# Expert 0's first product from the slot table of twelve tiles, with a branch that recomputes it, and weight loads placed in time by VectorE writes

## The chip, the cores and the metric

The kernel runs on one core of a Trainium2 chip. Five engines work from queues of their own and wait for one another through semaphores: TensorE (PE in the rows; its weight loads are PEld), VectorE (DVE), ScalarE (ACT), GpSimd (POOL) and SyncE (SP), which here only issues DMAs. An engine takes its instructions in the order in which the program gives them. The metric is the device time of one launch in microseconds (us).

## The reference, cut to what matters

Attention in chunks of 64 positions gives 2,304 tokens of 512 numbers. A first mixture of eight experts sends each token to the expert with the largest logit, in the order of the tokens, up to 576 for an expert. A second mixture, which takes most of the time, applies eight experts to every token.

```python
    x = np.ascontiguousarray(attn_out.transpose(0, 2, 1, 3)).reshape(B * S, H * D)
    ...
    logits = x @ w_gate
    expert_idx = np.argmax(logits, axis=1)
    ...
    for i in range(N):
        e = expert_idx[i]
        if counts[e] < capacity:
            disp[e, counts[e]] = x[i]
    ...
    h = np.maximum(np.einsum('ecd,edf->ecf', disp, w1), 0.0)
    y = np.einsum('ecf,efd->ecd', h, w2)
```

`w1[e]` is 512 x 1024 and `w2[e]` 1024 x 512. The next expert's input can't be known before the tokens have been routed.

## The kernel before, in words

The program is written out in the order in which each engine is to work (a manual schedule); nothing reorders it later. Where an operation's data isn't there, its engine waits, and everything behind it on that engine waits too.

**Attention and routing.** The loop `for n in range(NT + 6)` (NT = 18 tiles of 128 tokens) runs stages of several tiles interleaved: in iteration `n`, stage `f` works on tile `n - lag`. `order` lists the stages. Rows of attention output, split into a high and a low half of 16 bits, are written to the DRAM tensor `xs_d`, 512 numbers and eight more with the token's gate. After each group of three tiles (`G = 3`, six groups) `route(g)` gives the parts of the routing: one-hot of the chosen expert, `r_mm` (ranking by matmuls into the bank `p_tab`), `r_sel` to `r_ci`, rows and columns of a table, `r_tab` (three matmuls that put token numbers into slots) and `r_acc`, which adds them up in `tacc`. After the last group the sum becomes `gidx`, the list of tokens of each expert by slot, and `reg_i`, the counts and ranks.

**First mixture.** For expert `x`, `blocks(x, ...)` does 256 tokens at once: rows gathered from `xs_d` by indirect DMA on GpSimd's queue, turned, then a first product in four pieces of 24 matmuls (each matmul 256 columns), and a second product of 24 matmuls (512 columns) for each tile of 128 tokens. Weights and inputs are split into a high and a low half, so a product has three terms. Each piece is emptied from its PSUM bank by ScalarE (`hh`) and VectorE (`hl`); each tile of the second product by a square, a scale and a row write. The call with `main=True` does the first 256 tokens; the late block does tokens 256 to 511 where there are that many, behind `tc.If(rc > 256)`; the rest is a loop. `sites` are places in `blocks` (one behind each piece and one behind each tile) at which other work is put in.

**Weights.** Ahead of expert x's products its matrices "a" (`w1`) and "b" (`w2`) are loaded by `w_load` on SyncE's queue, their sizes are taken by `w_stat` ("a" by squares on ScalarE, "b" by maxima `wmxb` on VectorE), a common scale is made by `w_scale` (matmuls into `p_sum`) and `w_scale2`, and `w_split` writes high and low halves. Expert `x + 1` is split and the matrices of `x + 2` are measured while `x` runs. For expert 0, the loads of expert 1 are issued in iteration `NT + 1`, those of expert 2 ahead of `blocks(0, ...)`, and its late rows are turned (`xTc`) between first and second product (`between`).

Of the kernel before, what the change touches and what calls it, by code (L numbers as in the profile page):

```python
# [30 lines left out]
def kernel(ctx, tc, q, k, v, w_gate, w1, w2, capacity, w2_gate, w21, w22, out):  # L31
    nc = tc.nc
# [119 lines left out]
    def w_load(x, nm, h, nh=2):  # L152
# [152 lines left out]

    ohsum = [const.tile([128, E], F16, name=f"ohsum{j}") for j in range(2)]
# [4 lines left out]
    with ExitStack() as actx:  # L311
# [5 lines left out]
        ps_t = actx.enter_context(tc.tile_pool(name="ps_t", bufs=3, space=PSUM))  # L317
# [56 lines left out]
        def st_tr(i):  # L374
# [3 lines left out]
            for h2 in range(2):  # L378
                p = ps_t.tile([128, PR, 128], F32, tag="t", name="p_t")
# [29 lines left out]
        def st_dtr(i):  # L409
            d = T[i].pop("d")  # L410
            p = ps_t.tile([128, PR, 128], F32, tag="t", name="p_t")
# [51 lines left out]
        def st_xtr(i):  # L463
            p = ps_t.tile([128, KD, 128], F32, tag="t", name="p_t")
# [163 lines left out]
        for nm, ld, st, sc, sp in (("a", (2, 3), (3, 4, 5, 6), 6, (10, 13, 8, 15)), ("b", (9, 10), (11, 10, 12, 12), 12, (15, 14, 16, 17))):  # L628
            for h in range(2):
                plan(ld[h], lambda nm=nm, h=h: w_load(0, nm, h))  # L630
                plan(NT + 1, lambda nm=nm, h=h: w_load(1, nm, h))
# [4 lines left out]
            for h in range(4):  # L636
# [3 lines left out]
                 (st_max, 2), (st_xcopy, 4), (st_tr, 0), (st_pv, 3), (st_logits, 5), (st_dtr, 2))  # L640
        todo_r = {}
        for n in range(NT + 6):
# [9 lines left out]
            if i >= 0 and i % G == G - 1 and i < NT - G:  # L652
                for m, part in zip((n, n + 1, n + 1, n + 3, n + 5), route(i // G)):
                    todo_r.setdefault(m, []).append(part)
# [8 lines left out]
            for f, lag in order:  # L663
                i = n - lag
                if 0 <= i < NT:
                    f(i)
                for r in queue[:share]:
# [8 lines left out]
        for r in [gw, eps, rec, sel, pos, kx, rout, *second, *tab, tot1, tot2, racc]:  # L676
            r()

# [7 lines left out]
        nc.vector.tensor_copy(reg_i[:, 0:2 * E], p_tab[:, 256:256 + 2 * E])  # L686
    small_pool.pop()


    ps = ctx.enter_context(tc.tile_pool(name="ps", bufs=1, space=PSUM))  # L690
    turns = {"p": [0, 1, 2], "y": [3, 4], "c": [5, 6]}

    def in_turn(kind, shape, dtype, nm):
        i = turns[kind].pop(0)
        turns[kind].append(i)
        return ps.tile(shape, dtype, tag=f"m{i}", name=nm)

    with ExitStack() as cctx:
# [4 lines left out]
        sums["bank"] = ps.tile([128, 512], F32, tag="l", name="p_sum")  # L703
# [21 lines left out]
        def turn(rows, tag, bank="y"):  # L725
            xT = cp.tile([128, 2 * KD, 128 * len(rows)], F16, tag=tag, name=tag, bufs=2 if tag == "xT" else 1)
            for n, (idx, kg, xg) in enumerate(rows):
                p = in_turn(bank, [128, 2 * KD, 128], F16, "p_t")
                for kk in range(2 * KD):
                    nc.tensor.transpose(p[:, kk, :], xg[:, kk * 128:(kk + 1) * 128], id16)  # L730
                sl = slice(n * 128, (n + 1) * 128)
                nc.scalar.copy(out=xT[:, 0:KD, sl], in_=p[:, 0:KD])
                nc.vector.tensor_copy(xT[:, KD:2 * KD, sl], p[:, KD:2 * KD])
# [4 lines left out]
        def blocks(x, pre, nb, row0, sites=(), main=False, between=None):  # L738
            a, b = mats[x, "a"], mats[x, "b"]
# [14 lines left out]
            hh = cp.tile([128, KF, 256], F16, tag="hh", name="hh", bufs=1)[:, :, 0:W]  # L754
            hl = cp.tile([128, KF, 256], F16, tag="hl", name="hl", bufs=1)[:, :, 0:W]
            FG = 512 // W
            for fg in range(KF // FG):
                p = bank("p", [128, FG, W])
                for f4 in range(FG):
                    f = fg * FG + f4  # L760
                    n = 0
                    for w, lo in ((a.hi, 0), (a.hi, KD), (a.lo, 0)):
                        for kk in range(KD):
                            nc.tensor.matmul(p[:, f4, :], lhsT=w[:, kk, f * 128:(f + 1) * 128], rhs=xT[:, lo + kk, 0:W],  # L764
                                             start=(n == 0), stop=(n == 3 * KD - 1))
                            n += 1
                fs = slice(fg * FG, fg * FG + FG)
                nc.scalar.activation(out=hh[:, fs, :], in_=p, func=AF.Relu)
                nc.vector.scalar_tensor_tensor(out=hl[:, fs, :], in0=p, scalar=0.0, in1=hh[:, fs, :],
                                               op0=ALU.max, op1=ALU.subtract)  # L770
                site()
# [37 lines left out]
        def loads(x, nm, lo=0, hi=4):  # L809
            for h in range(lo, hi):  # L810
                w_load(x, nm, h, 4)
# [16 lines left out]
        first = gather(tokens(0, 0, 1))  # L828
        late = gather(tokens(0, 2, 3))
        rows = gather(tokens(1, 0, 1))  # L830
        for f in stats(1):
            f()
        pre = turn(first, "xT")

        for x in range(E):
            y = x + 1
            rc = nc.values_load(reg_i[0:1, x:x + 1], min_val=0, max_val=N)
# [9 lines left out]

            cur, pre = pre, turn_dma(rows) if y < E else None
            late_cur, late = late, gather(tokens(y, 2, 3)) if y < E else None
            rows = gather(tokens(y + 1, 0, 1)) if y + 1 < E else None  # L850
            if x == 0:
# [567 lines left out]
```

## Time and profile before

| | us |
|---|---|
| median of 3 runs | 1795.99 |
| the three runs | 1797.54, 1788.5, 1795.99 |
| the profiled execution | 1796.67 |
| its span, first to last instruction | 1795.0 |
| attention and routing, until gidx | 140.9 |
| first mixture, until its last second product | 413 |

[...] In rows with a time, the first number is the start in us from the span's start and the second the duration, or the stretch that several alike instructions fill; the bracket says how long the engine was idle before, and what ended that.

### The profile page before, as it was taken

How to read it: one execution, taken by the hardware profiler on the slowest of the kernel's cores; microseconds unless marked ns; L12 is line 12 of the kernel's file. 1: busy time of each engine (PE TensorE's matmuls, PEld its weight loads, DVE VectorE, ACT ScalarE, POOL GpSimd, SP SyncE). 2: the span in 40 equal slices, each digit the busy share in tenths (PEclk: the TensorE clock that was granted, in tenths of full speed). 3: DMA queues.
4: the chain of work that ended last, by engine and by line, in shares of the span. 5: the costliest groups of instructions: out<-in, count | busy, mean ns of one | idle time of the engine just before them, and what ended most of it. 6: DMA issues, size and time to landing. Idle time of an engine off the chain costs nothing.

```text
span 1795.0 us, 32982 instructions
## 1 busy us (share of the span) xinstructions
PE 1706.4 (95%) x13011; PEld 1234.3 (69%) x13011; DVE 1202.0 (67%) x2340; ACT 955.1 (53%) x1806; POOL 729.9 (41%) x754
## 2 busy tenths in 40 slices
PE   7887999988999999999999999999999999999995
PEld 6765667665555477777777777777777777777674
DVE  4897557756467666776678667677766786676652
ACT  7965557655245455564366445555643665453440
POOL 1345335542021345353455344453534553443432
PEclk9987999999999999999999999999999999999997
DMA  9747678943324322332324224223323142231200
GB/s 236 208 157 208 153 197 198 234 115 121 108 65 149 122 96 91 109 131 82 130 62 171 90 82 156 97 101 112 126 87 130 62 171 75 97 124 63 97 36 35
DMA packets 140902, 219.15 MB, mean 122 GB/s; under 512 B 62880, under 2 KB 81392, under 8 KB 140720
## 3 DMA queue, kind: packets, MB, share of 16 engines
q1 hardware_dynamic: 133728, 198.92, 35.1%
q0 software_dynamic: 5360, 17.24, 3.5%
q8 instruction: 115, 1.88, 0.4%
q10 hardware_dynamic: 1632, 0.56, 0.1%
q14 instruction: 67, 0.55, 0.1%
HBM read 167.56 MB, written 41.91 MB: 117 GB/s over the span
## 4 chain that ended last, share of the span: by engine, by line
PE 66%; DVE 7%; ACT 2%; DMA 1%; issue 1%; POOLq 0%; DVEq 0%; ACTq 0%
PE p_m L1122 35%; PE p_m L1210 27%; PE p_m L1254 3%; DVE wall L290 3%; ACT wall L289 1%; DVE acc L1189 1%; DMA wb_d<-wall 1%; DMA out_dram<-acc,rk 1%; DVE xsum L971 1%; DVE el L1130 1%; DVE tq L1137 0%; ACT eh L1127 0%; PE p_m L1010 0%; ACT tq L1162 0%; DVE wall L248 0%
## 5 line engine op out<-in xcount | busy, mean ns | idle before, releaser
L1122 PE MATMUL p_m<-x,wall 128*128 128x384 f16 x4032 | 669.6, 327 | 8.2 <-ACT tq L1162 4.9
L1210 PE MATMUL p_m<-wall,eh 128*128 128x256 f16 x3528 | 580.3, 273 | 0.0
L1122 PEld LDWEIGHTS <-wall 128*128 128x128 f16 x4032 | 394.8, 98 | 268.6 <-issue 15.2
L1134 POOL TENSOR_TENSOR el<-tq,eh 128x384 f16<-128x384 f32 x336 | 344.4, 1053 | 558.8 <-ACT eh L1127 558.6
L1210 PE MATMUL p_m<-wall,el 128*128 128x256 f16 x1764 | 481.0, 273 | 1.2 <-DVE el L1130 1.2
L1127 ACT ACTIVATE eh<-tq 128x384 f16<-128x384 f32 x540 | 273.9, 522 | 194.9 <-DVE tq L1140 102.8
L1210 PEld LDWEIGHTS <-eh 128*128 128x128 f16 x3528 | 344.3, 98 | 44.3
L1189 DVE SCALAR_TENSOR_TENSOR acc<-p_m,cf,acc 128x256 f32<-128x256 f32 (+1 forms) x378 | 175.1, 521 | 128.0 <-PE p_m L1210 128.0
L1137 DVE TENSOR_TENSOR tq<-p_m,tq 128x384 f32<-128x384 f32 x288 | 158.5, 556 | 138.4 <-PE p_m L1122 137.2
L1210 PEld LDWEIGHTS <-el 128*128 128x128 f16 x1764 | 172.6, 98 | 21.5 <-DVE el L1130 1.5
L1130 DVE SCALAR_TENSOR_TENSOR el<-tq,eh 128x384 f16<-128x384 f32 x204 | 175.7, 864 | 10.0 <-ACT eh L1127 8.6
L1140 DVE SCALAR_TENSOR_TENSOR tq<-tq 128x384 f32<-128x384 f32 x252 | 133.3, 554 | 2.9
L764 PEld LDWEIGHTS <-wall 128*128 128x128 f16 x1152 | 108.2, 101 | 30.5 <-issue 16.8
L1162 ACT COPY tq<-p_m 128x384 f32<-128x384 f32 x96 | 45.7, 476 | 111.1 <-PE p_m L1122 108.6
L764 PE MATMUL p_p<-xT,wall 128*128 128x256 f16 x768 | 90.6, 280 | 7.8 <-PEq L896 4.3
L268 POOL TENSOR_TENSOR tq<-stb 128x256 f32<-128x256 f32 x56 | 50.1, 895 | 90.3 <-DVE wsumsq L184 70.4
L1254 PE MATMUL p_m<-wall,eh 128*128 128x512 f16 x288 | 85.6, 379 | 0.0
L1175 ACT ACTIVATE tq<-tq 128x384 f32<-128x384 f32 x84 | 43.9, 523 | 69.9 <-DVE tq L1137 69.9
L289 ACT ACTIVATE wall<-stb,wsb 128x256 f16<-128x256 f32 (+1 forms) x56 | 31.3, 605 | 93.3 <-DMA wb_d<-wall 67.9
L268 POOL TENSOR_TENSOR tq<-sta 128x256 f32<-128x256 f32 x56 | 45.0, 804 | 76.8 <-DVE wall L290 44.3
L290 DVE SCALAR_TENSOR_TENSOR wall<-stb,wsb,wall 128x256 f16<-128x256 f32 (+1 forms) x56 | 38.4, 698 | 51.2 <-ACT wall L289 48.6
L240 POOL TENSOR_SCALAR stb<-stb,wsb 128x1024 f32<-128x1024 f32 x16 | 52.8, 3299 | 40.9 <-ACT wall L239 37.7
(261 smaller groups left out, 2133.2 us busy)
## 6 DMA issues: line engine op xcount, KB each, us to landing
x<-xt_d SPq DMA_DIRECT2D x147, 384.0 KB, 3.6
sta<-in_moe_w_dram SPq DMA_DIRECT2D x18, 1024.0 KB, 6.6
stb<-in_moe_w_dram SPq DMA_DIRECT2D x18, 1024.0 KB, 7.9
wb_d<-wall SPq DMA_DIRECT2D x20, 896.0 KB, 3.6
wall<-wb_d SPq DMA_DIRECT2D x20, 896.0 KB, 6.4
sta<-in_moe_w_dram SPq DMA_DIRECT2D x28, 512.0 KB, 8.0
stb<-in_moe_w_dram SPq DMA_DIRECT2D x28, 512.0 KB, 6.7
xt_d<-x SPq DMA_DIRECT2D x21, 384.0 KB, 3.6
```

Source lines behind the costliest of these rows:

```text
L268: nc.gpsimd.tensor_tensor(out=at(o), in0=at(u), in1=at(v), op=op)
L290: nc.vector.scalar_tensor_tensor(out=o[:, cs, 1], in0=src, scalar=m.s, in1=o[:, cs, 0], op0=ALU.mult, op1=ALU.subtract)
L764: nc.tensor.matmul(p[:, f4, :], lhsT=w[:, kk, f * 128:(f + 1) * 128], rhs=xT[:, lo + kk, 0:W], start=(n == 0), stop=(n == 3 * KD - 1))
L1122: nc.tensor.matmul(p, lhsT=wt[:, w, lw, kk, :], rhs=xt[:, lx, kk, :], start=first and n == 0, stop=n == 5, skip_group_check=not first)
L1127: nc.scalar.activation(out=hs[op][0][:, q, :], in_=src, func=AF.Relu if op in (A11, A12, A22) or plain else AF.Copy)
L1130: nc.vector.scalar_tensor_tensor(out=hs[op][1][:, q, :], in0=src, scalar=0.0, in1=hs[op][0][:, q, :], op0=ALU.max, op1=ALU.subtract)
L1134: nc.gpsimd.tensor_tensor(out=hs[op][1][:, q, :], in0=src, in1=hs[op][0][:, q, :], op=ALU.subtract)
L1137: nc.vector.tensor_tensor(out=o, in0=a, in1=b, op=ALU.add)
L1140: nc.vector.scalar_tensor_tensor(out=o, in0=a, scalar=0.0, in1=b, op0=ALU.max, op1=op)
L1189: nc.vector.scalar_tensor_tensor(out=acc[:, j, cols], in0=y, scalar=coefs[x][:, j:j + 1], in1=acc[:, j, cols], op0=ALU.mult, op1=ALU.add)
L1210: nc.tensor.matmul(bk.t[:, cols], lhsT=hs[op][lh][:, q, t * 128:(t + 1) * 128], rhs=b.q[q][:, w, lw, :], start=m in (1, 5) and q == 0 and ...
L1254: nc.tensor.matmul(y.t, lhsT=h[:, kk % 4, c * 128:(c + 1) * 128], rhs=w[:, kk, :], start=(n == 0), stop=(n == 3 * KF - 1))
```

## The change

Three things, all up to the last expert of the first mixture.

1. *The table of twelve tiles.* After the fourth of six groups (`EG = NG - 3`) its table is made in iteration 19 and not 20 to 22, `tacc` is cast to indices, and the rows of the first 256 slots of expert 0 are gathered from the part of `xs_d` that the first twelve tiles wrote. They are turned at the end of iteration NT + 3. The four pieces of expert 0's first product stand in iterations NT + 4 and NT + 5 and between the last steps of the routing. `first_product` and `turn_into` are the old code as functions, the first one a generator that gives the emptying of each piece as a call.
2. *The branch.* `e_count` keeps how many of the first 1,536 tokens chose expert 0. If that is at most 255, the first 256 tokens are done again, in two blocks of 128. So `blocks(0, ...)` has only the two sites behind the tiles of the second product; the splits of expert 1 and the measures of expert 2 are put there, and turning the late rows comes behind.
3. *The writes.* `w_load(..., behind_vector=True)` has VectorE write one column of the destination before the load, so that the load can't start before VectorE has come to that place. Loads of later experts are spread over the sites, one of 512 KB at a time.

```diff
+        if behind_vector:
+            nc.vector.memset(m.st[:, h * c, 0:1], 0.0)
         nc.sync.dma_start(out=m.st[:, h * c:(h + 1) * c, :],
...
+    early = wall[:, 2 * 4096:4 * 4096]
+    e_rows = [wall[:, t * 2 * XW:(t + 1) * 2 * XW].bitcast(F32) for t in range(2)]
+    EG = NG - 3
...
-                plan(NT + 1, lambda nm=nm, h=h: w_load(1, nm, h))
+                plan(NT + 3, lambda nm=nm, h=h: w_load(1, nm, h, 2, True))
...
+        def early_gather():
+            nc.vector.tensor_copy(e_idx, tacc[:, 0:2])
+            for j in range(2):
+                nc.gpsimd.indirect_dma_start(out=e_rows[j], out_offset=None, in_=xs_d[0:(EG + 1) * G * 128, :],
+                                             in_offset=bass.IndirectOffsetOnAxis(ap=e_idx[:, j:j + 1], axis=0))
...
+                if i // G == EG:
+                    kept_g, sum_g, out_g = last_g
+                    hooks[n + 2, st_lo] = [kept_g, out_g]
+                    hooks[n + 2, st_scores] = tab_g
+                    hooks[n + 2, st_max] = [sum_g, early_gather]
...
+            if n == NT + 3:
+                turn_into(e_xT, e_tokens, "p")
+                for j in range(2):
+                    nc.vector.tensor_copy(e_kg[:, j:j + 1], e_rows[j][:, DM:DM + 1])
+            if n >= NT + 4:
+                hidden.append(next(e_first))
...
-        for r in [gw, eps, rec, sel, pos, kx, rout, *second, *tab, tot1, tot2, racc]:
+        for r in [gw, eps, rec, sel, pos, kx, rout, *second]:
             r()
+        hidden.append(next(e_first))
+        hidden[0]()
+        for r in [*tab, tot1, tot2, racc]:
+            r()
+        hidden[1]()
+        hidden.append(next(e_first))
...
-            if x == 0:
-                for nm in "ab":
-                    loads(2, nm)
-            elif x + 2 < E:
-                loads(x + 2, "b", 0, 2)
...
-            behind = [lambda: loads(x + 3, "a", 0, 2)] if x + 3 <= E else [lambda: loads(E, "b")] if x == E - 2 else []
+            later = load(x + 3, "a", 0, 1, 2, 3) if x + 3 <= E else load(E, "b", 0, 1, 2, 3) if x == E - 2 else []
+            behind = later[:1]
...
+                    if x > 0:
+                        sites[h] += load(x + 2, "b", h)
...
+                if h in (1, 3):
+                    behind += later[h // 2 + 1:h // 2 + 2]
+            if x == 0:
...
+                every = [f for part in sites for f in part]
+                sites = [[*every[:8], *load(2, "a", 0, 1, 2, 3), next_rows], [*every[8:], *load(2, "b", 0, 1, 2, 3), *(f for f in behind if f not in later), *later]]
+                blocks(x, cur, 2, ranks(0), sites, True)
+                late, rows = ahead[0]
+                rc = count()
+                nxt = [turn(late_cur, "xTc", "p")]
+                known = nc.values_load(e_count[0:1, 0:1], min_val=0, max_val=N)
+                with tc.If(known <= 255):
+                    for t in range(2):
+                        blocks(x, turn(gather(tokens(0, t), "xgl", 1), "xTl", "c"), 1, lambda _, t=t: ranks(0)(t))
```

On VectorE, while expert 0 runs, this stands in the program before: splits of expert 1 (`sta_1811`, `stb_1815`), the copies of the late rows, the emptying of the second product's first tile, and the maxima of expert 2's matrix.

```order
L248 SCALAR_TENSOR_TENSOR wall<-sta_1811,wsa,wall 128x1024
L769 SCALAR_TENSOR_TENSOR hl<-p_p,hh 128x512
L248 SCALAR_TENSOR_TENSOR w_3_2148<-stb_1815,wsb,w_2_2147 128x1024 x2
L733 COPY xTc<-p_t 128x4x128 x2
L89 TENSOR_SCALAR x2h<-ssq_2351 128x1
L90 TENSOR_SCALAR x2s<-x2h 128x1
L92 TENSOR_SCALAR x2i<-x2h 128x1
L791 SCALAR_TENSOR_TENSOR row_2359<-p_y,x2s,row_2359 128x2x256
L797 SCALAR_TENSOR_TENSOR rkt<-xg,x2i,iw 128x1
L170 TENSOR_REDUCE wmxb<-stb_2141 128x1 x4
```

Here the copies stand ahead of both tiles' emptying and of the maxima. In the changed kernel the same engine has, from behind the splits of expert 1's first matrix on (its second is `stb_1949`), with expert 2's matrices as `sta_2303` and `stb_2371` and expert 3's first one as `sta_2393`:

```order
L158 MEMSET sta_2303 128x1 x4
L89 TENSOR_SCALAR x2h<-ssq_2347 128x1
L90 TENSOR_SCALAR x2s<-x2h 128x1
L92 TENSOR_SCALAR x2i<-x2h 128x1
L859 SCALAR_TENSOR_TENSOR row_2355<-p_y,x2s,row_2355 128x2x256
L865 SCALAR_TENSOR_TENSOR rkt<-e_kg,x2i,iw 128x1
L250 SCALAR_TENSOR_TENSOR w_3_2229<-stb_1949,wsb,w_2_2228 128x1024 x2
L158 MEMSET stb_2371 128x1 x4
L172 TENSOR_REDUCE wmxb<-stb_2371 128x1 x4
L158 MEMSET sta_2393 128x1 x4
L906 TENSOR_LOAD reg_i
L334 COPY xTc<-p_t 128x4x128 x2
```

The copies have moved behind the second tile's emptying, the splits, the maxima of expert 2 and all the small writes; the maxima stand directly behind the writes that let their loads go.

On SyncE's queue for expert 0 this stands before: turned rows of expert 1, all loads of expert 2, then the row writes of the two tiles.

```order
L721 DMA_TRANSPOSE xT<-xg 128x8x128 x2
L157 DMA sta_2135<-in_moe_w_dram 128x1024 x4
L157 DMA stb_2141<-in_moe_w_dram 128x2x512 x4
L794 ISA
L794 DMA x_d<-row_2359 128x512
L799 ISA
L799 DMA rk_d<-rkt 128x2
```

In the changed kernel it has:

```order
L805 DMA_TRANSPOSE xT<-xg 128x8x128 x2
L862 ISA
L862 DMA x_d<-row_2268 128x512
L867 ISA
L867 DMA rk_d<-rkt 128x2
L159 DMA sta_2303<-in_moe_w_dram 128x1024 x4
L862 ISA
L862 DMA x_d<-row_2355 128x512
L867 ISA
L867 DMA rk_d<-rkt 128x2
L159 DMA stb_2371<-in_moe_w_dram 128x2x512 x4
L159 DMA sta_2393<-in_moe_w_dram 128x1024 x4
```

The loads of expert 2 have moved behind the first and the second tile's row writes, and those of expert 3 stand directly behind them.

## Rows read from the trace of the kernel before

**Rows 1.** The page: engines' busy time, and the chain that ended last.

```profile
PE 1706.4 (95%) x13011; PEld 1234.3 (69%) x13011; DVE 1202.0 (67%) x2340; ACT 955.1 (53%) x1806; POOL 729.9 (41%) x754
...
PE 66%; DVE 7%; ACT 2%; DMA 1%; issue 1%; POOLq 0%; DVEq 0%; ACTq 0%
```

**Rows 2.** Windows of 5 us: busy time of each engine, granted clock, DMA.

```profile
core 0: us, PE busy (x) PEld busy (x) DVE busy (x) ACT busy (x) POOL busy (x), PEclk, DMA share, GB/s
...
135.00:140.00 5.00, 1.04 (x13) 0.67 (x13) 4.58 (x24) 4.55 (x9) 1.99 (x3) 0.50 0.38 112
...
145.00:150.00 5.00, 2.97 (x21) 2.30 (x22) 2.15 (x4) 1.17 (x2) 3.78 (x4) 0.50 0.73 204
150.00:155.00 5.00, 5.00 (x30) 3.69 (x29) 0.06 (x1) 0.60 (x1) 3.89 (x5) 0.59 0.67 167
```

**Rows 3.** TensorE in order of time, 135 to 184 us.

```profile
135.51 0.17 PE L516 MATMUL p_tab<-goh,tri 128*128 128x8 f16 x1 [2.31 <-DVE goh L510]
...
146.11 1.01 PE L730 MATMUL p_t<-id,xg 128*128 128x128 f16 x8 [4.52 <-DMA xg<-xs_d,gidx]
...
149.08 5.20 PE L764 MATMUL p_p<-xT,wall 128*128 128x256 f16 x24 [0.67 <-ACT xT L732]
...
154.47 8.02 PE L764 MATMUL p_p<-xT,wall 128*128 128x256 f16 x72
...
163.43 0.59 PE L781 MATMUL p_y<-wall,hh 128*128 128x512 f16 x2
...
173.79 10.64 PE L764 MATMUL p_p<-xTc,wall 128*128 128x256 f16 x96
```

**Rows 4.** VectorE in order of time, 123 to 176 us.

```profile
123.82 0.69 DVE L406 TENSOR_TENSOR d<-p_s,mx 128x512 f32<-128x512 f32 x1
...
135.28 0.18 DVE L510 TENSOR_TENSOR goh<-ioef,gix 128x24 f16<-128x24 f32 x1
...
140.60 0.30 DVE L577 TENSOR_TENSOR gidx<-tacc,p_tab 128x144 int32<-128x144 f32 x1 [0.62 <-PE p_tab L570]
...
155.55 0.15 DVE L205 TENSOR_REDUCE wmma<-p_sum 128x1 f32<-128x4 f32 x1
...
163.46 1.96 DVE L248 SCALAR_TENSOR_TENSOR wall<-sta,wsa,wall 128x1024 f16<-128x1024 f32 x1 [0.52 <-ACT wall L247]
...
165.94 2.73 DVE L248 SCALAR_TENSOR_TENSOR w<-stb,wsb,w 128x1024 f16<-128x1024 f32 x2
168.59 0.74 DVE L733 COPY xTc<-p_t 128x512 f16<-128x512 f16 x2
...
171.43 4.59 DVE L170 TENSOR_REDUCE wmxb<-stb 128x1 f32<-128x1024 f32 x4
```

**Rows 5.** GpSimd in order of time, 161 to 168 us.

```profile
161.39 2.94 POOL L241 TENSOR_TENSOR w<-stb,w 128x1024 f16<-128x1024 f32 x1
164.32 3.81 POOL L240 TENSOR_SCALAR stb<-stb,wsb 128x1024 f32<-128x1024 f32 x1
```

**Rows 6.** Groups by line: busy time, mean ns of one, idle time before.

```profile
L769 DVE SCALAR_TENSOR_TENSOR hl<-p_p,hh 128x512 f16<-128x512 f32 x44 | 30.2, 688 | 35.6 <-ACT hh L768 35.6
L768 ACT ACTIVATE hh<-p_p 128x512 f16<-128x512 f32 x44 | 25.8, 586 | 37.3 <-PE p_p L764 33.3 <-DVEq L896 2.2 <-DVE row L791 1.7
```

**Rows 7.** Loads of 1 MB (page), and the tile stb's loads, 100 to 250 us.

```profile
stb<-in_moe_w_dram SPq DMA_DIRECT2D x18, 1024.0 KB, 7.9
...
L157 SPq DMA_DIRECT2D stb<-in_moe_w_dram x14: 368/467/569, 116.6 to 237.7; - x14
...
DMA to landing us min/median/max: 3.9/6.8/12.5
```

**Rows 8.** TensorE behind branches, 340 to 385 us, and one window.

```profile
348.15 4.12 PE L764 MATMUL p_p<-xT,wall 128*128 128x256 f16 x21 [2.95 <-PEq L896]
...
379.67 4.74 PE L764 MATMUL p_p<-xTc,wall 128*128 128x128 f16 x56 [4.92 <-issue]
...
380.00:385.00 5.00, 5.00 (x59) 4.64 (x57) 0.69 (x1) 1.15 (x2) 0.99 (x2) 0.72 0.40 144
```

More of the change, by code (lines that the diff above doesn't have):

```diff
@@ L463, in st_xtr @@
         def st_xtr(i):
-            p = ps_t.tile([128, KD, 128], F32, tag="t", name="p_t")
+            p = in_turn("p", [128, KD, 128], F32, "p_t")
             for kk in range(KD):
@@ L666 @@
                     f(i)
+                for r in hooks.pop((n, f), ()):
+                    r()
                 for r in queue[:share]:
@@ L686 @@
         nc.vector.tensor_copy(reg_i[:, 0:2 * E], p_tab[:, 256:256 + 2 * E])
+        for f in hidden[2:]:
+            f()
     small_pool.pop()
[L690 to L696, printed above, removed]
+    banks[1] = ctx.enter_context(tc.tile_pool(name="ps_b", bufs=1, space=PSUM))
     with ExitStack() as cctx:
@@ L702 @@
         second_of_odd.append(xw)
-        sums["bank"] = ps.tile([128, 512], F32, tag="l", name="p_sum")
+        sums["bank"] = banks[1].tile([128, 512], F32, tag="l", name="p_sum")
         for x in range(2, E + 1, 2):
@@ L726, in turn @@
             xT = cp.tile([128, 2 * KD, 128 * len(rows)], F16, tag=tag, name=tag, bufs=2 if tag == "xT" else 1)
[L727 to L733, printed above, removed]
+            turn_into(xT, rows, bank)
             return xT, rows
         def blocks(x, pre, nb, row0, sites=(), main=False, between=None):
-            a, b = mats[x, "a"], mats[x, "b"]
+            b = mats[x, "b"]
             xT, rows = pre
@@ L753, in blocks @@
                 nc.gpsimd.tensor_copy(to[:, 1:2].bitcast(I32), idx)
[L754 to L771, printed above, removed]
+            if x == 0 and main:
+                hh, hl = e_hh, e_hl
+            else:
+                hh = cp.tile([128, KF, 256], F16, tag="hh", name="hh", bufs=1)[:, :, 0:W]
+                hl = cp.tile([128, KF, 256], F16, tag="hl", name="hl", bufs=1)[:, :, 0:W]
+                for hidden in first_product(x, xT, hh, hl, W, lambda shape: bank("p", shape)):
+                    hidden()
+                    site()
             for t in range(nb):
@@ L807, in stats, with load @@
             return [f for p in zip(each(w_stat, x, "a", 4, True), each(w_stat, x, "b", 4, False)) for f in p]
-        def loads(x, nm, lo=0, hi=4):
-            for h in range(lo, hi):
-                w_load(x, nm, h, 4)
+        def load(x, nm, *hs):
+            return [lambda h=h: w_load(x, nm, h, 4, True) for h in hs]
         head = []
@@ L826, in tokens, with count @@
             return [gidx[:, x, t:t + 1] for t in ts]
-        first = gather(tokens(0, 0, 1))
+        for f in stats(1):
+            f()
+        pre = (None, e_tokens)
         late = gather(tokens(0, 2, 3))
         rows = gather(tokens(1, 0, 1))
-        for f in stats(1):
-            f()
-        pre = turn(first, "xT")
         for x in range(E):
             y = x + 1
-            rc = nc.values_load(reg_i[0:1, x:x + 1], min_val=0, max_val=N)
+            def count():
+                return nc.values_load(reg_i[0:1, x:x + 1], min_val=0, max_val=N)
+            if x > 0:
+                rc = count()
             rank_engine = mybir.EngineType.Activation if x == E - 1 else mybir.EngineType.SP
@@ L846, in ranks, with rows_ahead @@
                 return lambda t: rb if t0 + t == 0 else rank(t0 + t)
+            def rows_ahead():
+                return gather(tokens(y, 2, 3)) if y < E else None, gather(tokens(y + 1, 0, 1)) if y + 1 < E else None
             cur, pre = pre, turn_dma(rows) if y < E else None
-            late_cur, late = late, gather(tokens(y, 2, 3)) if y < E else None
-            rows = gather(tokens(y + 1, 0, 1)) if y + 1 < E else None
-            if x == 0:
-                for nm in "ab":
-                    loads(2, nm)
-            elif x + 2 < E:
-                loads(x + 2, "b", 0, 2)
+            late_cur = late
+            if x > 0:
+                late, rows = rows_ahead()
             if x == E - 1:
@@ L1045 @@
     P = ep.tile([128, NT, E], F32, name="P")
-    p_lb = ps.tile([128, 512], F32, tag="l", name="p_l")
+    p_lb = banks[1].tile([128, 512], F32, tag="l", name="p_l")
     p_l = p_lb[:, 0:NT * 2 * E].rearrange("p (j c) -> p j c", c=2 * E)
```

80 lines of the change are left out of this document (67 added, 13 removed).

## Prediction

> **What bounds the kernel now.** I read the page first: TensorE is busy for 95% of the span, and the chain of work that ended last is 66% TensorE, so over the whole run time is saved where TensorE waits [rows 1]. [...]
>
> **Step 1: the second product starts earlier.** Expert 0's first 256 rows come from the table of twelve tiles, so its four pieces of 24 matmuls no longer wait for gidx. The gather is let go in iteration 19, behind the subtraction that ends at 124.5 there and one table update; before, 5.5 us passed from gidx to the first turned row (140.60 to 146.11), so these rows are there between 130.5 and 132.5 (the gather also waits for the write of the gate), and are turned by 133, when the work of iteration NT+3 is done [rows 3, 4]. On GpSimd's queue the two gathers go ahead of a row write and the fifth group's columns, which wait for VectorE's routing anyway. Two things push the routing back. On VectorE, ahead of the last group's one-hot (135.28), stand two copies of turned rows (0.74 for the pair, as at 168.59) and eight small operations (two casts, four writes, two copies of the gate) at 0.15 each, as at 155.55 [rows 4]: 1.9 us, of which some fits into idle gaps; I take 1.6 (bounds 0 and 3), so the one-hot is at 136.9. On TensorE the first piece stands ahead of the ranking. At the full clock 24 matmuls are 24 x 8.02/72 = 2.7 us, at the low one 5.2 [rows 3]. With rows turned and copied I expect them from 134.6 to 137.3, ranking at 137.4. Pieces two and three (5.3 us) stand between the ranking and the last table: table at 143.0. The table-to-gidx step is short, gidx about 143.5 against 140.60. Piece four ends at 146.1 and the second product starts at 146.3: 17.1 us earlier than 163.43. At the low clock for the first piece it is 149.0, a gain of 14.4. Each piece is emptied by one ScalarE and one VectorE operation of 0.59 and 0.69 us [rows 6]; the last of them ends near 147.7.
>
> **Step 2: one small wait inside the second product.** Before, a tile of it takes (173.79 - 163.43)/2 = 5.2 us [rows 3]. Expert 1's scale now stands between its two tiles, and needs four maxima on VectorE, 4.59 us as at 171.43 [rows 4], which start at 147.7: they end at 152.3, when the first tile has been done since 151.5. TensorE waits 0.8, the second tile runs from 152.6 to 157.8. Expert 1's weights, held back to iteration NT+3, are asked for at about 133.5; loads of 1 MB land after 7.9 us at the median [rows 7], before 147.7. That is the cover; a landing that is later delays everything behind it by as much. On SyncE's queue these 4 MB now stand ahead of the last two tiles' row writes, and so of the gathers that wait for them (late block, expert 1): needed at 158 and later, which leaves ten us.
>
> **Step 3: the late block now waits for VectorE.** This is the term that decides. In the order shown above, the copies of the late block's rows stand behind everything that belongs to expert 1's splits and, new, behind the four maxima of expert 2's second matrix. Those wait for loads that four small VectorE writes let go only just ahead of them. Before, scale and splits took from 155.55 to 168.67, 13.1 us, with three emptyings of 0.69 among them [rows 4, 6]. After, those go (-2.1), and the emptying of the second tile comes in: for the first tile it took from about 168.6 (163.43 + 5.2) to 171.43, 2.8 us [rows 3, 4]; the small writes add 0.5. So 14.3 us. It starts when the first tile has been emptied behind the maxima, 152.3 + 2.1 = 154.4, and ends at 168.7. Then the loads of 512 KB: the fastest landed in 3.9 us, the median in 6.8, the slowest in 12.5 [rows 7]. The first can be read at 172.6, the last, issued some 1.5 us later, at 177.0; four maxima of 1.15 then end at 178.0 (177.2 if loads are quick, 182.4 if the last is as slow as the slowest). Writes and copies add 1.2. The late block starts at 179.2, where it started at 173.79: **5.4 us later**, although the second product was 17.1 earlier. TensorE has nothing else from 159 to 179.
>
> **Step 4: the clock.** Behind the hole at 141 to 146 the granted clock was 0.50 and 24 matmuls took 5.2 us in place of 2.7 [rows 2, 3]. The new hole is longer, so I add 2.5 us: the late block ends 7.9 us later than before. The emptying of its pieces has two banks and a VectorE that is free again, so nothing more is lost there.
>
> **Step 5: the loads of experts 1 to 6 are spread.** In two places before, TensorE stands at a branch: 2.95 us at 348.15 and 4.92 us at 379.67, and the window behind the second is granted 0.72 [rows 8]. Both lie right behind a burst of weight loads. Spread loads can give back at most the 7.9 us and some 2 of clock, 10 in all, and at least nothing; but the queue that issues them still stands behind the turning of rows by DMA, and of the burst ahead of the second gap three loads in four still come together. I take 2.5. The writes themselves are 8 of 0.15 us for each expert on an engine that isn't waited for there.
>
> **The sum.** +7.9 - 2.5 = +5.4 us on the profiled execution, 1796.67 us (span 1795.0): 1802.1, say **1802**. The three runs shown had a median of 1795.99 and went from 1788.5 to 1797.54, so this is 0.3% above the median. About 0.5%, 9 us, is what a measurement of this kernel can tell from no change.
>
> [...] VectorE's two splits of expert 1's second matrix run beside GpSimd's scaling of its other half. At 163.46 a split took 1.96 us beside the GpSimd operation that ended at 164.33; but at 165.94 two took 2.73 us, 1.37 each, under one that lasted from 164.32 to 168.13 [rows 4, 5]. [...]
>
> **Rivals.** *Slower* (0.35): step 3 is right but larger. It decides once the late block starts after 182.8 (that is 173.79 + 9, the 2.5 of clock and of step 5 cancelling). Two things reach it: the last load of expert 2 lands in 12.5 us and not 6.8 (+4.2), or the first piece runs at the low clock (+2.7) and a split or two is held by GpSimd (+2). Together 1811. For it: landings under a burst do reach 12.5 us [rows 7], and gathers, row writes and expert 3's loads fall in the same 20 us. Against: the bursts of 4 MB that stood there before are gone.
>
> *Faster* (0.2): the late block isn't held by expert 2's maxima, or only briefly, and the spread loads remove both branch gaps. Were the copies free at 168.7, it would start at 170: -3.8 + 2.5 - 10 = -11.3, 1785. For it: the gaps of rows 8 are real and follow loads. Against: VectorE executes in order, and the loads can't land before they are asked for. If only the gaps went, it would be 1796.67 + 7.9 - 10 = 1795, the same.
>
> *The branch costs by itself* (within the chances above): all engines now test a count and jump over the recomputation. On TensorE the worst stand behind a branch is 4.92 us [rows 8]; it would add that, 1807, if it came on the path, but the test stands where TensorE waits some 20 us for VectorE's copies, so I count 0. [...]
>
> *The table of twelve doesn't do* (0.01): if expert 0 had fewer than 256 tokens in the first 1,536, two blocks would be recomputed, each at least 96 matmuls of 128 columns (4.74/56 = 0.085 us each [rows 8]) and a tile of 5.2: 13.3 us each, 1829 or more. With the reference's inputs 320 of the first 1,536 tokens choose expert 0.
>
> **How the numbers follow.** Same (0.45) is the forecast, 1794 to 1805; slower reaches to 1815, and faster to 1785. Leaving out a tenth at each side gives 1788 to 1814; the forecast's own range is 1795 to 1806.
>
> **What would show it.** Right: four groups of matmuls of the first product between 134 and 146; the second product at 146 to 149; TensorE idle from about 159 to 179 with VectorE ending it, VectorE itself waiting for expert 2's loads; a low clock behind it; smaller gaps at the branches of experts 5 and 6. Wrong: a late block that starts before 174, or gaps at the branches that are gone entirely, or a second product later than 152.

## The result, and the profile after

The changed kernel is slower: 1811.87 us in the median of 4 runs (1811.68 to 1815.91) against 1792.97 of the kernel before in the same set (4 runs), a ratio of 1.0109 (95%: 1.0088 to 1.0129). The profiled execution took 1811.91 us, and its span is 1810.2. The forecast was 1802 and "the same"; what came true is its rival *slower*, at its place (the late block) and nearly with its sum (1811).

The page of the changed kernel, as [rows 1]:

```profile
PE 1707.7 (94%) x13011; PEld 1235.1 (68%) x13011; DVE 1204.0 (67%) x2404; ACT 956.0 (53%) x1806; POOL 727.6 (40%) x754
...
PE 66%; DVE 6%; ACT 2%; DMA 1%; issue 1%; POOLq 0%; ACTq 0%; DVEq 0%
```

Busy times hardly differ from before (TensorE +1.3 us), so nearly all of the 15.2 us of span are waiting, not work. Windows of the changed kernel, as [rows 2]:

```profile
135.00:140.00 5.00, 5.00 (x25) 3.75 (x26) 2.98 (x14) 0.94 (x2) 0.00 (x0) 0.50 0.97 372
140.00:145.00 5.00, 5.00 (x53) 4.40 (x52) 3.49 (x18) 1.19 (x2) 2.09 (x3) 0.95 1.01 349
...
165.00:170.00 5.00, 0.00 (x0) 0.00 (x0) 2.39 (x4) 4.49 (x5) 3.45 (x2) 0.50 1.12 292
170.00:175.00 5.00, 0.00 (x0) 0.00 (x0) 2.86 (x5) 1.71 (x3) 5.00 (x2) 0.50 1.09 323
175.00:180.00 5.00, 0.00 (x0) 0.00 (x0) 0.00 (x0) 3.85 (x8) 2.95 (x4) 0.50 1.08 360
```

The hole at 135 to 150 of [rows 2] is filled, but from 135 to 140 at a granted clock of 0.50 of full speed; a new hole, with TensorE at 0 for whole windows, lies at 165 to 185, and the DMA share is 1.08 to 1.12 until 180. TensorE of the changed kernel in order of time, as [rows 3]:

```profile
135.70 5.12 PE L346 MATMUL p_p<-wall 128*128 128x256 f16 x24
...
141.07 5.40 PE L346 MATMUL p_p<-wall 128*128 128x256 f16 x48
...
146.50 2.78 PE L346 MATMUL p_p<-wall 128*128 128x256 f16 x24
...
149.58 5.34 PE L849 MATMUL p_y<-wall 128*128 128x512 f16 x24 [0.29 <-DVE reg_i L774]
...
160.71 1.06 PE L331 MATMUL p_t<-id,xg 128*128 128x128 f16 x16
187.28 12.80 PE L346 MATMUL p_p<-xTc,wall 128*128 128x256 f16 x96 [25.51 <-DVEq L979]
```

The second product starts at 149.58 (before 163.43, 13.9 earlier), the late block at 187.28 (before 173.79, 13.5 later), and its four pieces take 12.80 in place of 10.64. L979 is the new branch; a q behind an engine's name means its sequencer, under which the trace lists the branch (8.4 us on TensorE's, 0.07 on VectorE's; SPq is SyncE's queue). VectorE ahead of it, as [rows 4]:

```profile
159.44 4.87 DVE L250 SCALAR_TENSOR_TENSOR wall<-sta,wsa,wall 128x1024 f16<-128x1024 f32 x4 [0.27 <-ACT wall L249]
...
168.49 4.34 DVE L250 SCALAR_TENSOR_TENSOR w<-stb,wsb,w 128x1024 f16<-128x1024 f32 x2 [2.23 <-ACT w L249]
172.78 0.08 DVE L158 MEMSET stb<- 128x1 f32 x4
180.69 1.22 DVE L172 TENSOR_REDUCE wmxb<-stb 128x1 f32<-128x1024 f32 x1 [7.83 <-DMA stb<-in_moe_w_dram]
182.54 3.83 DVE L172 TENSOR_REDUCE wmxb<-stb 128x1 f32<-128x1024 f32 x3 [0.63 <-DMA stb<-in_moe_w_dram]
...
186.32 0.42 DVE L334 COPY xTc<-p_t 128x512 f16<-128x512 f16 x1
...
186.66 0.42 DVE L334 COPY xTc<-p_t 128x512 f16<-128x512 f16 x1
```

GpSimd beside the b splits, as [rows 5], and the loads of 160 to 190 us with their median to landing, as [rows 7]:

```profile
166.47 2.85 POOL L242 TENSOR_SCALAR stb<-stb,wsb 128x1024 f32<-128x1024 f32 x1 [3.68 <-ACT w L241]
169.40 2.35 POOL L243 TENSOR_TENSOR w<-stb,w 128x1024 f16<-128x1024 f32 x1
```

```profile
sta<-in_moe_w_dram SPq DMA_DIRECT2D x8, 512.0 KB, 7.6
stb<-in_moe_w_dram SPq DMA_DIRECT2D x4, 512.0 KB, 9.3
```

This is step 3 as told, splits, writes, maxima that wait for their loads, copies, only each later. But two things end at 187: the copies (187.08) and VectorE's passing of the branch (186.4 to 187.1), and the trace names the second. The profile alone can't tell which of them TensorE needs. From here on the delay stays about the same: expert 1's first product starts at 211.53 (before 195.97, +15.6), and the span is 15.2 longer. At the two places of [rows 8] TensorE now waits 2.19 and 3.39 us, where before it waited 2.95 and 4.92:

```profile
366.64 2.78 PE L346 MATMUL p_p<-xT,wall 128*128 128x256 f16 x24 [2.19 <-PEq L987]
...
394.81 3.41 PE L346 MATMUL p_p<-xTc,wall 128*128 128x128 f16 x58 [3.39 <-issue]
```

### The profile page after: what moved, and what is told of

Read it like the earlier page. It is cut to its first block, busy times and chain, and to the rows that moved or that the text cites. A ratio compares the mean times of both kernels' runs of the same rounds, so it can differ in the third digit from the quotient of the medians.

```text
span 1810.2 us, 33118 instructions
## 1 busy us (share of the span) xinstructions
PE 1707.7 (94%) x13011; PEld 1235.1 (68%) x13011; DVE 1204.0 (67%) x2404; ACT 956.0 (53%) x1806; POOL 727.6 (40%) x754
## 4 chain that ended last, share of the span: by engine, by line
PE 66%; DVE 6%; ACT 2%; DMA 1%; issue 1%; POOLq 0%; ACTq 0%; DVEq 0%
PE p_m L1213 35%; PE p_m L1301 28%; PE p_m L1345 3%; DVE wall L292 3%; ACT wall L291 1%; DVE acc L1280 1%; DMA out_dram<-acc,rk 1%; DVE xsum L1062 1%; DVE el L1221 0%; DMA wb_d<-wall 0%; DVE tq L1228 0%; DMA x_d<-row 0%; ACT eh L1218 0%; PE p_m L1101 0%; ACT tq L1253 0%
## 5 line engine op out<-in xcount | busy, mean ns | idle before, releaser
L346 PE MATMUL p_p<-xT,wall 128*128 128x256 f16 x672 | 77.8, 276 | 7.9 <-PEq L987 3.6
L170 ACT ACTIVATE wsq<-sta 128x1024 bf16<-128x1024 f32 x64 | 67.4, 1054 | 6.2 <-issue 3.7
```

## The experiments

The runs came in four sets, in which the kernel before had medians of 1795.05, 1801.46, 1800.18 and 1800.84. So kernels are compared by the ratio to the kernel before of their own set, and places in a trace as distances from the start of expert 0's second product, S, since S itself moves from run to run.

**Set 1.** *Loads early*: expert 2's loads back where they stood.

```
-  [*every[:8], *load(2, "a", 0, 1, 2, 3), next_rows], [*every[8:], *load(2, "b", 0, 1, 2, 3), ...
+  [*every[:8], next_rows], [*every[8:], ...
+  else:                       # x == 0, ahead of blocks(0, ...)
+      w_load(2, nm, h, 4)     # "a" and "b", h = 0 to 3, without VectorE's write
```

> The changed kernel with expert 2's eight loads put back to where they stood, ahead of expert 0's second product and without VectorE's writes. Theory 'late loads': the late block stands behind the maxima of expert 2, and these behind loads that are let go only at 172.8; with the loads queued on SP behind the transposes (about 162) they have landed by about 174, the maxima follow the b splits without a wait (172.8 to 177.7), the two copies to 178.5, and the late block begins at 178 to 180 where it began at 187.28: 8 us less, about 1803 to 1805. Rival 'branch': what holds TensorE is the branch at L979 and its code, or the splits; then the late block begins within 1.5 us of 187.3 and the time stays at 1810 to 1812.

It took 1805.73 us, a ratio of 1.0067 (95%: 1.0039 to 1.0094). The late block starts at 182.76, that is S + 32.1 (changed kernel S + 37.7), and VectorE still waits 3.05 us for the loads. The result lies between the two theories: late loads are about 5.6 us of the late block's delay, no more.

```profile
182.76 12.14 PE L346 MATMUL p_p<-xTc,wall 128*128 128x256 f16 x96 [19.94 <-DVEq L983]
```

*Copies first*: the turning of the late rows ahead of the b splits.

```
-  [*every[8:], ...
+  [lambda: nxt.append(turn(late_cur, "xTc", "p")), *every[8:], ...
-  nxt = [turn(late_cur, "xTc", "p")]    # was behind blocks(0, ...)
```

> The changed kernel with the late block's copies ahead of the b splits of expert 1 and of the maxima of expert 2, the loads as they are in the changed kernel. Theory 'place of the copies': the copies follow the emptying of the second tile (166.2), so the late block's first product begins at 167 to 168, 20 us sooner; but its third piece needs a bank that VectorE empties only behind the maxima, which end at 186 to 187, so the first product ends at 193 to 195 where it ended at 200.1: 5 to 7 us less, about 1805 to 1807. Rival 'branch': TensorE waits until about 187 all the same, time 1810 to 1812. Rival 'place alone': the start of the late block is the whole of the loss, 1793 to 1796.

It took 1810.26 us, a ratio of 1.0093 (1.0056 to 1.0129). VectorE and then TensorE of this kernel:

```profile
160.62 0.75 DVE L334 COPY xTc<-p_t 128x512 f16<-128x512 f16 x2
163.91 2.90 DVE L250 SCALAR_TENSOR_TENSOR w<-stb,wsb,w 128x1024 f16<-128x1024 f32 x2 [2.54 <-ACT w L249]
166.75 0.08 DVE L158 MEMSET stb<- 128x1 f32 x4
179.88 5.16 DVE L172 TENSOR_REDUCE wmxb<-stb 128x1 f32<-128x1024 f32 x4 [13.04 <-DMA stb<-in_moe_w_dram]
```

```profile
185.40 13.29 PE L346 MATMUL p_p<-xTc,wall 128*128 128x256 f16 x96 [28.91 <-DVEq L979]
```

The copies end at 161.4, and TensorE still waits 24 us more, until VectorE has done the maxima and passed the branch. From S this start is even later than the changed kernel's (S + 41.4 against S + 37.7). My theory of the copies' place, and the forecast's step 3 with it, is refuted as the whole of the wait.

*Both edits*:

> Both edits on the changed kernel: expert 2's loads early and the late block's copies ahead of splits and maxima. Theory 'late loads and place of the copies': late block from 167 to 168, maxima at VectorE's end by about 178 to 179, third piece from there, first product's end at 183 to 186 where it was 200.1: 14 to 17 us less, 1795 to 1798, no better than the kernel before although the second product ends 14 us sooner. Rival 'early product pays': no wait between the pieces, first product's end at 178 to 180, 1788 to 1791. Rival 'branch': over 1805.

It took 1806.15 us, a ratio of 1.0065 (1.0041 to 1.0088), which is no better than loads early alone. The copies are done at 163.8, but the late block starts at 180.12 (S + 33.6), after TensorE has stood idle until VectorE's branch. The rival *branch* holds.

```profile
180.12 12.88 PE L346 MATMUL p_p<-xTc,wall 128*128 128x256 f16 x96 [21.46 <-DVEq L983]
```

*Spreading alone*: on the kernel before, only the held and spread loads of experts 3 to 8.

> The kernel before with one part of the change alone: the loads of experts 3 to 8 spread and held by VectorE's writes, nothing else. Forecast's step 5: 0 to 10 us less, 2.5 as the value taken, 1790 to 1793 by the starts of the late experts (before 348.15 and 379.67 in the rows). Rival 'nothing': the gaps stay or move, within 1 us of the kernel before. Rival 'writes late': a write stands behind VectorE's other work and its load lands late, over 1796.

It took 1797.81 us, a ratio of 1.0013 (0.9996 to 1.003). TensorE at the places of [rows 8], and a third:

```profile
329.98 7.94 PE L766 MATMUL p_p<-xT,wall 128*128 128x256 f16 x56 [3.73 <-issue]
...
350.43 2.78 PE L766 MATMUL p_p<-xT,wall 128*128 128x256 f16 x24 [1.26 <-PEq L902]
...
379.77 3.29 PE L766 MATMUL p_p<-xTc,wall 128*128 128x128 f16 x56 [3.87 <-issue]
```

The two gaps shrink by 1.7 and 1.1 us, but TensorE now stands for 3.73 at 329.98, where the kernel before showed 0.58 at 327.44. The rival *nothing* holds: spreading gives nothing that can be measured.

**Set 2.** What in the branch holds TensorE? In the program, the skipped block uses the two PSUM banks of the late block, and its emptying is VectorE's. The idea, a guess at this point, is that TensorE's wait for VectorE as the last reader of those banks ends only when VectorE is past the block, whether it runs or is skipped. *No block*: both edits, the recomputation left out.

```
-  with tc.If(known <= 255):
-      for t in range(2):
-          blocks(x, turn(gather(tokens(0, t), "xgl", 1), "xTl", "c"), 1, ...)
```

> As the kernel with both edits (loads early, copies first), and the conditional recomputation left out with its branch (its table always holds 256 tokens of expert 0 in this run, so nothing is computed less). Seen so far: with both edits the copies ended at 163.8, and TensorE still began the late block at 180.12, right behind VectorE's passing of the branch. Theory 'wait on skipped code': the late block's matmuls write the two banks that the skipped block uses as well, so they wait until VectorE has passed the branch, and VectorE comes there only behind the maxima (179.8). Without the block the late block begins at 164 to 165, its third piece waits for a bank until about 180.5, and its first product ends at 185 to 187 where it ended at 193: 6 to 8 us less, 1797 to 1800. Rival 'something else on VectorE' (the maxima or the register loads): start stays at about 180, 1804 to 1807.

It took 1805.57 us, a ratio of 1.0028 (1.0013 to 1.0043). The late block starts at S + 16.8, and its third piece waits for VectorE's emptying, which stands behind the maxima:

```profile
166.35 7.70 PE L346 MATMUL p_p<-xTc,wall 128*128 128x256 f16 x48 [4.61 <-ACT xTc L333]
183.42 7.70 PE L346 MATMUL p_p<-xTc,wall 128*128 128x256 f16 x48 [9.37 <-DVE hl L352]
```

So the wait goes with the block (4.61 us idle ahead of the late block, 21.46 with both edits). The first product ends at 191.1, later than the 185 to 187 expected, in part because S is 3 us later here than with both edits.

*Other banks*: both edits, the block kept, with `bank` `"p"` and `"y"` in place of `"c"`.

> As the kernel with both edits, the conditional recomputation kept, but in the banks of the first and second product of the main block instead of the two banks of the late block. Theory 'wait on skipped code': what holds TensorE is the shared banks, not the branch; the late block begins when TensorE has passed the branch itself (165.6 with both edits) and ends its first product at 185 to 187: within 2 us of the kernel without the block, 1797 to 1801. Rival 'branch': a branch makes every engine wait for all others, start at about 180, 1804 to 1807.

It took 1810.36 us, a ratio of 1.004 (1.002 to 1.0061). That is 0.25% less than both edits, which the intervals don't tell from nothing; the places in the trace do tell. TensorE:

```profile
156.14 1.06 PE L331 MATMUL p_t<-id,xg 128*128 128x128 f16 x16
162.06 8.34 PE L346 MATMUL p_p<-xTc,wall 128*128 128x256 f16 x48 [4.87 <-PEq L983]
...
183.04 8.09 PE L346 MATMUL p_p<-xTc,wall 128*128 128x256 f16 x48 [12.64 <-DVE hl L352]
```

The late block starts at S + 17.7, where both edits with shared banks had S + 33.6: only the banks differ. So it is the shared banks, not the branch as such. But the gain ends after two pieces: the third needs a bank that VectorE empties behind the maxima, and the first product ends at 191.1 (185 to 187 was expected).

*Maxima late*: other banks, and expert 2's maxima and squares moved behind the late block.

> As the kernel with the other banks, and the maxima and sums of squares of expert 2 moved behind the late block. Theory: nothing is left between the copies and the late block's emptying on VectorE, so the late block begins at 165 to 167 and its four pieces run without a wait, 10.6 to 12.8 us, to 177 to 180 (before: 184.27); the moved maxima may hold expert 1's sums by 0 to 3 us; 1788 to 1794, that is 2 to 7 us under the kernel before. Rival 'given back': the maxima now hold expert 1's first product and the splits of expert 2 by as much, 1795 to 1800.

It took 1804.43 us, a ratio of 1.0019 (1.0001 to 1.0037). Now the late block runs without a break from 162.99 and expert 1 starts at 187.15, 8.8 us sooner than in the trace of before. TensorE then:

```profile
187.15 2.78 PE L346 MATMUL p_p<-xT,wall 128*128 128x256 f16 x24 [1.19 <-issue]
195.65 0.59 PE L179 MATMUL p_sum<-wmxa,ones 128*128 128x4 f32 x2 [5.73 <-ACT wsq L170]
```

The sums wait for the moved squares, and expert 2 starts 34.0 us behind expert 1, where the kernel before needs 23.2. *Given back*, as the rival said.

*Maxima late, no block*:

> As the kernel with the maxima late, without the conditional recomputation and its branch. Theory: the branch costs TensorE 5 to 8 us from the end of its transposes, of which the copies cover all but 1 or 2; start at 164 to 165, within 3 us of the kernel with the maxima late. Rival 'the branch has a price of its own': 5 us or more less than that.

It took 1804.42 us, a ratio of 1.0022 (1.0005 to 1.0039), which is the same. In the kernel with the block TensorE's branch took 3.9 us (158.0 to 161.9), hidden behind the copies, and the late block starts at S + 16.7 in both.

**Set 3.** *Maxima inside*: as maxima late, but the four maxima and squares are a site of the late block, behind its fourth piece.

```
   with tc.If(rc > 384) as cmp:
-      blocks(x, (late_t, late_r), 2, ranks(2))
+      blocks(x, (late_t, late_r), 2, ranks(2), [[], [], [], sums_ahead])
```

> As the kernel with the other banks, but the maxima and sums of squares of expert 2 stand inside the late block, behind its fourth piece (and in each other arm of its condition). With the maxima behind the whole late block, expert 1's first product began at 187.15, but its sums then waited 5.73 for ScalarE's squares, and expert 2 came only at 221.14, 34.0 us after expert 1 where the kernel before takes 23.2. Theory 'place of the maxima': VectorE and ScalarE do them from 177 to 182, beside the late block's second product, so expert 1 still begins at 186 to 189 and expert 2 at 210 to 214 (before: 219.20): 1787 to 1793 beside a kernel before at 1795, a ratio of 0.995 to 0.999. Rival 'row buffers': ScalarE still stands 6 us for the buffer of a row (187.91) and expert 2 comes at 216 or later, ratio 1.000 to 1.003.

It took 1803.96 us, a ratio of 1.0029 (1.0008 to 1.0051). The maxima are hidden (187.72 to 192.3, beside the second product) and the sums don't wait. But the late block starts at S + 22.7, 5.4 us behind its copies, and expert 1 at 199.32 (186 to 189 was expected). The late block's line in this kernel, and the branch's (duration in ns and start, on TensorE's sequencer):

```profile
173.01 13.43 PE L346 MATMUL p_p<-xTc,wall 128*128 128x256 f16 x96 [10.53 <-PEq L983]
...
L983 PEldq COMPARE_BRANCH  x1: 9585/9585/9585, 162.9 to 162.9; - x1
```

*With four row buffers* (`bufs=4` for the tile `row`):

> The same with four buffers in place of three for the rows that are written back. Theory 'row buffers': ScalarE's wait of about 6 us for the first row of the late block goes, expert 1 and 2 begin 1 to 6 us sooner than with three buffers. Theory 'place of the maxima': within 1.5 us of the kernel with three buffers.

It took 1803.15 us, a ratio of 1.0008 (0.9984 to 1.0032). The late block starts at S + 22.0 and expert 1 at S + 48.7 (49.0 with three buffers), so the buffers of the rows aren't it.

```profile
171.68 13.48 PE L346 MATMUL p_p<-xTc,wall 128*128 128x256 f16 x96 [9.84 <-PEq L983]
```

**Set 4.** *Maxima inside, no block* (four row buffers):

> As the kernel with the maxima inside the late block and four row buffers, without the conditional recomputation and its branch. In the two kernels before this one TensorE's branch over the skipped block took 9.6 and 9.0 us, and the late block began 22.7 and 22.0 us behind the second product, 4 to 5 us behind its copies. Theory 'the branch's own time': without it the late block begins 16 to 17.5 us behind the second product and expert 1 43 to 45 us behind it (49.0 and 48.7 with the branch): 4 to 6 us less than with the branch, a ratio of 0.996 to 0.999 to the kernel before. Rival 'given back': the copies, the clock or the loads of expert 2 take its place, ratio 1.000 to 1.003.

It took 1800.9 us, a ratio of 1.0003 (0.9981 to 1.0025). The late block starts at S + 16.7 and expert 1 at S + 43.3, as the first theory said: the branch costs 5 us here.

```profile
165.19 7.76 PE L346 MATMUL p_p<-xTc,wall 128*128 128x256 f16 x48 [4.11 <-ACT xTc L333]
```

The ratio is the rival's: expert 2 starts at 215.00 (before 219.20), but the last second product of expert 7 at 404.1 (before 402.6). TensorE stands in between for 2.02 us at 228.9, 2.14 at 349.0 and 6.44 at 380.4, so at no single place. All its stands there add up to 20.9 us, against 14.7 in the kernel before; those marked `issue`, which the last section comes back to, are 3.9 of the 6.3 more. Why a lead of 4 us doesn't live through experts 2 to 7 I haven't settled beyond that. The traces also come from executions that differ by some us, and the interval of the ratio leaves room for a gain of 3.4.

*No GpSimd*: the changed kernel, all b splits of expert 1 on ScalarE and VectorE.

```
-  w_split(y, nm, h, 4, 2 * (nm == "b" and h > 1))
+  w_split(y, nm, h, 4, 2 * (x > 0 and nm == "b" and h > 1))
```

> The changed kernel with all four b splits of expert 1 on ScalarE and VectorE, none on GpSimd. Forecast's step 3 (rival) had 2 us for splits held by GpSimd. Theory 'GpSimd slows them': VectorE's b splits took 2.17 each beside GpSimd's subtractions; alone they take 1.2 to 1.3 each, the four of them 5 where two took 4.34, so the writes of expert 2's loads move by less than 1.5 us, the late block begins at 186 to 190 and the time stays at 1809 to 1814: the contention is real and worth nothing here, since the two splits saved come back as two more. Rival 'VectorE is slow there for another reason': 2.0 or more each, four take 8, late block at 190 or later, 1814 to 1818.

It took 1822.9 us, more than the 1809 to 1814 expected, but the kernel before was also 8 us slower in this set; the ratio, 1.014 (1.0097 to 1.0183), isn't told apart from the changed kernel's 1.0109. VectorE, and SyncE's queue:

```profile
165.50 4.87 DVE L250 SCALAR_TENSOR_TENSOR w<-stb,wsb,w 128x1024 f16<-128x1024 f32 x4 [0.16 <-ACT w L249]
170.32 0.08 DVE L158 MEMSET stb<- 128x1 f32 x4
180.71 1.22 DVE L172 TENSOR_REDUCE wmxb<-stb 128x1 f32<-128x1024 f32 x1 [10.30 <-DMA stb<-in_moe_w_dram]
```

```profile
159.74 0.74 SPq L862 DMA_DIRECT2D x_d<-row  x1
...
163.45 1.91 SPq L159 DMA_DIRECT2D sta<-in_moe_w_dram  x4
172.06 0.35 SPq L862 DMA_DIRECT2D x_d<-row  x1
...
173.16 2.71 SPq L159 DMA_DIRECT2D stb<-in_moe_w_dram  x4
```

SyncE's queue in the changed kernel:

```profile
172.13 0.35 SPq L862 DMA_DIRECT2D x_d<-row  x1
...
173.22 2.97 SPq L159 DMA_DIRECT2D stb<-in_moe_w_dram  x4
```

Four splits take about what two took (1.22 each against 2.17), so the contention is real. The writes come sooner than in the changed kernel (170.32 against 172.78, which is S + 21.6 against S + 23.2), yet the loads go out at 173.16, no sooner than there (S + 24.5 against S + 23.6). What stands ahead of them on SyncE is the write of the second tile's row (172.06), which waited 6.5 us for the first row to land (5.3 in the changed kernel).

## Why the prediction was wrong, by its steps

*Step 1* (second product at 146.3, or 149.0 with the first piece at the low clock): it started at 149.58. The first piece took 5.12 us at a granted clock of 0.50. The piece isn't always slow: the same code up to there took 2.92, 2.92 and 2.91 for it in copies first, other banks and maxima late (windows of 130 to 140 at 1.00 in the first two), and 4.52 to 5.14 in the nine others. The term was sized for the lucky case, and that is worth 2.2 us.

*Step 2* (0.8 us inside the second product): 0.25. Right.

*Step 3* (late block at 179.2) is the step that failed. Its mechanism is what the trace shows, VectorE in order behind maxima that wait for loads, but three of its terms were too small. Of the 8.1 us between 179.2 and 187.28, 4.1 had come up by the writes that let the loads go (168.7 forecast, 172.8 measured): 2.9 already as the maxima of expert 1 began (147.7 forecast, 150.64 measured), most of it step 1's slow piece; 1.6 from the two b splits, which took 4.34 where 2.73 was taken; and 0.4 less from the rest. The other 4.0 are the loads: the first maximum was forecast 3.9 us behind the writes and began 7.9 behind them. The first load landed 7.4 us after its issue, where the forecast took 3.9, the fastest landing of the kernel before, and the last one 9.3 where it took 6.8, with DMA at 1.08 to 1.09 in the windows of 170 to 180. The row write ahead of the loads on SyncE's queue, which the forecast didn't count, held them for only 0.4 of this (issued at 173.22). But *no GpSimd* shows that it would have been the later of the two had the writes come sooner.

The forecast also took the copies for the only thing TensorE waits for. *Copies first* and *other banks* show a second wait of about the same length, on the banks that the skipped block shares. It added nothing to this result, because the copies ended at 187.08, but with it left in, earlier copies bring nothing.

*The rival slower* named the three terms: the first piece at the low clock (+2.7, measured 2.2), a split held by GpSimd (+2, measured 1.6) and late loads (+4.2, measured 4.0). No run shows the +2 itself: the two b splits took 1.6 more than the 2.73 taken for them, and four without GpSimd took 1.22 each. That the rival's sum came so near is in part luck. It let the last load land in 12.5 us, which by step 3's own times (last load issued 1.5 us behind the first, landed at 177.0 with 6.8) is +5.7, not +4.2, and the maxima's end 183.9, not 182.4.

*Step 4* (clock, +2.5): 12.80 against 10.64, +2.2, at a mean granted clock of 0.82 from 187.2 to 200.1 where the late block before had 1.00. Right.

*Step 5* (spread loads, -2.5): nothing, 1.0013 (0.9996 to 1.003). Wrong in size; the bound of nothing held. The second of its two gaps (4.92 us at 379.67) isn't at a branch either: in the kernel before TensorE had run 40 of that block's matmuls, from 372.35 on, when it stood. That bursts of loads cause the gaps wasn't shown; what comes ahead of TensorE's going on there is a transfer of instructions, by 1.3 us (last section).

*The sum.* It came out as +13.5 for the start of the late block, +2.2 for its clock and -0.5 for the rest, against +5.4, +2.5 and -2.5.

*The branch* was counted as 0 because it stood where TensorE waits anyway. In the changed kernel that was so: 161.2 to 169.6, under a wait until 187. It cost 5 us once the wait was gone (maxima inside, with and without the block), about the 4.92 that the forecast named as the worst, though that row is no branch. The traces show a transfer of instructions inside each jump of 3.9 to 9.6 us, 1.4 to 1.6 us ahead of its end (last section).

*The splits beside GpSimd*: *no GpSimd* has 1.22 against 2.17 us for a split. But 2.17 stands for one of 1.29 and one of 3.14. The first split began beside GpSimd's TENSOR_SCALAR (166.47 to 169.32) and took no longer than the 1.37 of before; the second began under its TENSOR_TENSOR (169.40 to 171.75) and ended 1.1 us behind it. The two rows that the prediction set against each other differ in the same way: the split of 1.96 us lay under a TENSOR_TENSOR and ended 1.1 us behind it, and the two of 1.37 under a TENSOR_SCALAR [rows 4, 5]. So in these rows a split beside GpSimd's TENSOR_TENSOR takes 1.96 and 3.14 us, and one beside its TENSOR_SCALAR 1.29 to 1.37. Why isn't shown.

## What to carry to other kernels

In this program code that is skipped still takes part in waits: TensorE's next use of two banks waited until VectorE had walked past a block that never ran, 21.46 us idle against 4.87 with other banks. So give a block that almost never runs PSUM banks that nothing behind it needs soon. When work is moved ahead, follow what stood between it and the next step on each queue, and size what you find there by the rows that the new order makes likely, not by the best ones. Here the 14 us won on TensorE were lost behind VectorE, which took its instructions in the program's order, and the loads that it waited for (7.83 us ahead of the first maximum, then 0.63). In the best kernel (without the block) the second product starts 15.0 us sooner than before and expert 1 4.2 us sooner, and nothing that can be measured is left at the end (ratio 1.0003). Before placing a write that is to release a load, look at what stands ahead of the load on its queue: in *no GpSimd* the writes came 1.6 us sooner behind S than in the changed kernel and the loads 0.9 later, behind a row write.

## What was not expected of the hardware

TensorE's jump over the skipped block took 3.9 us where it began at 158.0 (maxima late), 4.8 at 156.2 and 156.8 (copies first, other banks), 6.7 at 158.8 (both edits), and 7.9 to 9.6 where it began at 161.2 or later. The jumps of the other engines at the same line took 0.05 to 0.07 us.

The DMA records of the traces show a transfer that goes with the jump. In all nine kernels with the block one transfer of 16 KB, of a queue marked `instruction` (q8), runs inside the jump, and the jump ends 1.4 to 1.6 us behind it. In the changed kernel the jump lasts from 161.18 to 169.62 and the transfer from 167.24 to 168.18; its line here is from the `--dma` view of 167.2 to 168.2, and the views of 161.2 to 167.2 and of 168.3 to 169.7 have none:

```profile
L979 PEldq COMPARE_BRANCH  x1: 8437/8437/8437, 161.2 to 161.2; - x1
...
q8 instruction: 1, 0.02, 5.9%
```

The transfer itself takes 0.9 to 1.4 us; what the jumps differ in most is how late it starts, 1.0 us after the jump's start in maxima late and 7.1 in maxima inside. Three stands marked `issue`, for which the profile shows no wait, go with such transfers too: in the kernel before TensorE goes on at 379.67 [rows 8], 1.3 us behind one, at 329.98 of spreading alone 1.4 behind one, and at 380.4 of maxima inside, no block 1.5 behind one.

Why the transfer starts late isn't shown. In the six jumps of 6.7 us and more the loads of expert 2 go out during the jump, and in the three shorter ones only as it ends or behind it. But in the same six the DMAs that turn expert 1's rows (L805) were issued 2.4 to 6.0 us before the jump began, and in the three shorter ones at its start or behind it. No run separates the two.
